# Two x tiles and two slices of w1 as four 128 KB loads, taken up tile by tile at the start of a Mish layer

## The chip, the cores and the metric

The kernel runs on one core of a Trainium2 chip. The metric is the time of one execution on the device, in microseconds (us). The profile is one further execution, recorded by the hardware profiler; its span runs from the first instruction to the last.

## What is computed

```python
B, S, D, F = 1, 2048, 512, 1792          # all bfloat16
def reference(x, w1, b1, w2):
    h = jnp.einsum("bsd,df->bsf", x, w1) + b1
    sp = jnp.log1p(jnp.exp(-jnp.abs(h))) + jnp.where(h > 0, h, jnp.zeros_like(h))
    act = h * jnp.tanh(sp)               # Mish
    return jnp.einsum("bsf,fd->bsd", act, w2)
```

## The kernel before, in words

The two products work on tiles of 128. D is 4 tiles (index k), F is 14 tiles (f), S is 16 tiles of x (i or j) in four blocks of 512 rows (s). For the first product TensorE holds a 128 x 128 piece of w1 as weights and streams a block of x transposed (xT, D on the partitions) past it; four such products, k 0 to 3, add up in one of the eight PSUM banks. ScalarE then applies Mish with the bias b1 (`mish`, L194) and writes `a_sb`. The second product (`mm2`, L245) holds a piece of `a_sb` as weights and streams w2 past it over all 14 f; VectorE copies the result out (L231), SP's queue stores it (L235). VectorE also works out the last six rows of x's first product as dot products (L208).

Everything is ordered by hand. A `Stream` is an engine with a semaphore: `mark` counts up when an instruction ends, and `wait` puts a wait ahead of the engine's next instruction. Each load has a semaphore of its own (`load`, L91 to L94).

The loads are all issued at the top, from two queues. SP issues, in this order: `x_nat` (x tiles 0 and 1 in one load of 256 KB, L129; each partition takes two neighbouring rows of x, 2 KB together), w1's k 2 and 3 for f 0 to 3, w1's k 0 and 1 and then k 2 and 3 for f 4 to 7, a transposing load of x tiles 2 and 3 (L132), w1 for f 8 to 13 in two loads, and then w2, the six rows for VectorE, a transposed copy of w1 and the rest of x by transposing loads. ScalarE's queue issues w1's k 0 and 1 for f 0 to 3 (256 KB, L134), then b1 (L135), and after these the table load for Mish (L150).

x tiles 0 and 1 are transposed on TensorE. While their load is under way, TensorE runs fillers: products of constants into a bank that is not yet used, five of 512 and five of 128 columns (`WARM`, L7; `dummy`, L156). Then `transpose_x` (L163) runs three times: k 0 into bank 6, k 1 into bank 5, k 2 and 3 into bank 4, each for both tiles (eight transposes, L168). After each, VectorE copies the bank into `xT` (L172: 256, 256 and 512 columns). VectorE then turns b1 into a column per f (L256 to L261).

The first products follow (L262 to L265): for f 0 to 3 and then f 4 to 7, over k 0 to 3, products of 256 columns (x tiles 0 and 1) into banks 0 to 7 (`mm1_step`, L190). L266 to L269 add x tiles 2 and 3 for the same eight f and hand each to Mish. Then come f 8 to 13 of block 0 with 512 columns, the second product of block 0, and the same for the other blocks.

Since a partition of `x_nat` holds two neighbouring rows of x, output tiles 0 and 1 are stored through a view with the same interleaving (`out01`, L128 and L234).

Of the kernel before, what the change touches and what calls it, by code (L numbers as in the profile page):

```python
# [4 lines left out]

P = 128
WARM = (512,) * 5 + (128,) * 5  # L7
GROUPS = ((0, 4), (4, 8), (8, 14))
BLOCKS = (512, 512, 512, 512)
LAST = (0, 256, 416, 512)  # L10
# [25 lines left out]
def bass_standalone__dense_activation_mish__prompt_kernel(  # L36
# [10 lines left out]
    BF, F32 = dt.bfloat16, dt.float32  # L47
# [3 lines left out]
    KT, FT = D // P, F // P  # L51
    assert (S, D, F) == (2048, 512, 1792) and sum(BLOCKS) == S
    x2, out2 = x[0], out[0]
# [5 lines left out]
    with ExitStack() as es:  # L59
        def sb(name, shape, t):  # L60
            return es.enter_context(nc.sbuf_tensor(name, shape, t))

        x_nat = sb("x_nat", [P, 2, D], BF)
        xT = sb("xT", [P, KT, S], BF)
# [9 lines left out]
        o_sb = sb("o_sb", [P, S // P, D], BF)  # L74
# [5 lines left out]
        ps = es.enter_context(nc.psum_tensor("ps", [P, 8, 512], F32))  # L80

        def sem(name):
            return es.enter_context(nc.semaphore(name))

        sp = Stream(nc.sync, None)
        pe = Stream(nc.tensor, sem("c_pe"))
        dve = Stream(nc.vector, sem("c_dve"))
        act = Stream(nc.scalar, sem("c_act"))
        pool = Stream(nc.gpsimd, sem("c_pool"))

        def load(q, dst, src, name, transpose=False):  # L91
            s = sem(name)
            (q.eng.dma_start_transpose if transpose else q.eng.dma_start)(dst, src).then_inc(s, 16)
            return (s, 16)  # L94

        t_w1, t_w2, t_xT, t_w1T, t_xv = {}, {}, {}, {}, {}

        def load_w1(q, ks, a, b):
            t = load(q, w1_sb[:, ks, a * P:b * P], w1v[:, ks, a * P:b * P], "s_w1_%d_%d" % (ks.start, a))
            for f in range(a, b):  # L100
                for k in range(ks.start, ks.stop):
                    t_w1[k, f] = t
# [6 lines left out]
        def load_xT(lo, hi):  # L109
            t = load(sp, xT[:, :, lo:hi], x2[lo:hi, :], "s_xT%d" % lo, True)  # L110
            for j in range(lo // P, hi // P):
                t_xT[j] = t
# [11 lines left out]
        t_bz = dve.mark(nc.vector.memset(b1_pad[:, :], 0.0))  # L124
        act.wait(t_bz)

        x01 = x2[0:2 * P, :].rearrange("(p j) d -> p j d", j=2)
        out01 = out2[0:2 * P, :].rearrange("(p j) d -> p j d", j=2)  # L128
        t_xn = load(sp, x_nat[:, :, :], x01, "s_xn")  # L129
        for a, b in GROUPS:  # L130
            if a == F0:
                load_xT(2 * P, 4 * P)  # L132
            for ks in (slice(0, 2), slice(2, KT)):
                load_w1(act if (a, ks.start) == (0, 0) else sp, ks, a, b)  # L134
        t_b1 = load(act, b1_nat[:, :], b1.rearrange("(j p) -> j p", p=P), "s_b1")  # L135
        load_w2(0, 5)
        load_w2(5, FT)
# [5 lines left out]
        for s in range(2, len(BLOCKS)):  # L143
# [4 lines left out]
        t_id = pool.mark(pool.eng.affine_select(ident[:, :], ones[:, :], pattern=[[1, P]], compare_op=ALU.is_equal,  # L148
                                                fill=0.0, base=0, channel_multiplier=-1))
        act.eng.preload_act_table(ACT.Mish)  # L150

        c_w = nc.const_aps.tensor(1.0, [P, P], BF)
        c_m = nc.const_aps.tensor(1.0, [P, 512], BF)

        def dummy(n):
            nc.tensor.matmul(ps[:, 7, 0:n], c_w, c_m[:, 0:n], start=True, stop=True)  # L156

        free = [[] for _ in range(8)]
        t_cp = {}
        t_mish = {}  # L160


        def transpose_x(bank, ks):  # L163
            pe.wait(t_xn, t_id, *free[bank])
            psb = ps[:, bank, :].bitcast(BF)
            for i, k in enumerate(ks):
                for j in range(2):
                    mm = nc.tensor.transpose(psb[:, (2 * i + j) * P:(2 * i + j + 1) * P],  # L168
                                             x_nat[:, j, k * P:(k + 1) * P], ident[:, :])
            n = len(ks)  # L170
            dve.wait(pe.mark(mm))
            t = dve.mark(nc.vector.tensor_copy(xT[:, ks[0]:ks[0] + n, 0:2 * P],  # L172
                                               psb[:, 0:2 * n * P].rearrange("p (k t) -> p k t", k=n)))
            for k in ks:
                t_cp[k] = t
            free[bank] = [t]

        def width(s):
            return BLOCKS[s] - (NV if s == len(BLOCKS) - 1 else 0)

        def mm1_step(s, f, k, bank, j0=0, j1=None):
            j1 = BLOCKS[s] // P if j1 is None else j1
            lo, hi = j0 * P, min(j1 * P, width(s))
            first = k == 0 and j0 == 0
            if first:
                pe.wait(*free[bank])
            pe.wait(t_w1[k, f])
            for j in range(starts[s] // P + j0, starts[s] // P + j1):
                pe.wait(t_cp[k] if j < 2 else t_xT[j])
            return nc.tensor.matmul(ps[:, bank, lo:hi], w1_sb[:, k, f * P:(f + 1) * P],  # L190
                                    xT[:, k, starts[s] + lo:starts[s] + hi], start=first,
                                    stop=(k == KT - 1 and hi == width(s)))
# [28 lines left out]
        s_out = sem("s_out")  # L221
        n_out = 0

        def put(i, lo, hi, bank, t_mm, q):
            nonlocal n_out
            if q is act:
                act.wait(t_mm)
                t = act.mark(act.eng.activation(o_sb[:, i, lo:hi], ps[:, bank, 0:hi - lo], ACT.Copy))  # L228
            else:
                dve.wait(t_mm)  # L230
                t = dve.mark(nc.vector.tensor_copy(o_sb[:, i, lo:hi], ps[:, bank, 0:hi - lo]))  # L231
            free[bank] = [t]
            q.wait(t)
            dst = out01[:, i, lo:hi] if i < 2 else out2[i * P:(i + 1) * P, lo:hi]  # L234
            q.eng.dma_start(dst, o_sb[:, i, lo:hi]).then_inc(s_out, 16)  # L235
            n_out += 1

        t_v = None
# [1 line left out]
        def mm2(i, lo, hi, bank, q=sp):  # L240
            s = max(b for b in range(len(BLOCKS)) if starts[b] <= i * P)
            pe.wait(*free[bank])
            for f in range(FT):
                pe.wait(t_w2[f], t_mish[s, f], t_v if i == S // P - 1 else None)
                mm = nc.tensor.matmul(ps[:, bank, 0:hi - lo], a_sb[:, f, i * P:(i + 1) * P], w2_sb[:, f, lo:hi],  # L245
                                      start=(f == 0), stop=(f == FT - 1))
            put(i, lo, hi, bank, pe.mark(mm), q)


        for n in WARM:  # L250
            dummy(n)
        transpose_x(6, (0,))
        transpose_x(5, (1,))
        transpose_x(4, (2, 3))
        dve.wait(t_b1, t_bz)
        t_b1p = dve.mark(nc.vector.tensor_copy(b1_pad[0:FT, :], b1_nat[:, :]))  # L256
        dve.wait(t_b1p)
# [2 lines left out]
        dve.wait(t_b1t)  # L260
        t_b1c = dve.mark(nc.vector.tensor_copy(b1_sb[:, :], b1_t[:, 0:FT]))  # L261
        for a, b in GROUPS[:2]:  # L262
            for k in range(KT):
                for f in range(a, b):
                    mm1_step(0, f, k, f, 0, 2)  # L265
        for f in range(F0):  # L266
            for k in range(KT):
                mm = mm1_step(0, f, k, f, 2, 4)
            mish(0, f, f, pe.mark(mm))  # L269

        for s in range(len(BLOCKS)):
            for f in range(F0 if s == 0 else 0, FT):
                bank = f % 8 if s == 0 else 4 + f % 4
                for k in range(KT):
                    mm = mm1_step(s, f, k, bank)
                mish(s, f, bank, pe.mark(mm))
            for i in range(starts[s] // P, starts[s + 1] // P):
                if i < S // P - 1:
                    mm2(i, 0, D, i % 4)
                    dots(DOTS[i])  # L280
                    if i == S // P - 3:
                        t_v = mish_v()
                else:
                    for n in range(len(LAST) - 1):
                        mm2(i, LAST[n], LAST[n + 1], (i + n) % 4, act if LAST[n + 1] == D else sp)
# [29 lines left out]
```

## Time and profile before

| | |
|---|---|
| time, median of 3 runs | 105.08 us (104.6 to 105.33) |
| time of the profiled execution | 104.52 us |
| its span | 103.2 us |
| TensorE (PE) busy | 100.1 us, 97% |
| VectorE (DVE) busy | 64.8 us, 63% |
| ScalarE (ACT) busy | 39.1 us, 38% |
| moved by DMA | 10.58 MB |

PE is TensorE's products, PEld its weight loads, which run beside them. A timeline row has the start, the length, the engine, the kernel's line, the operation with what it writes and reads, and how many instructions are merged in it; in brackets stands the idle time ahead of it and what ended that. A chain row has the start, the length and what ran. In the list of groups, the number behind x is the count, then come busy time, mean length in ns, and the idle time ahead. A row of the windows gives the stretch, its length, the busy time of each engine with its count of instructions, then the granted clock of TensorE, the busy share of the 16 DMA engines, and GB/s. A product's length includes the time that it takes to run through the array, so products overlap; their pitch, from start to start, is what counts.

### The profile page before, as it was taken

How to read it: one execution, taken by the hardware profiler on the slowest of the kernel's cores; microseconds unless marked ns; L12 is line 12 of the kernel's file. 1: busy time of each engine (PE TensorE's matmuls, PEld its weight loads, DVE VectorE, ACT ScalarE, POOL GpSimd, SP SyncE). 2: the span in 40 equal slices, each digit the busy share in tenths (PEclk: the TensorE clock that was granted, in tenths of full speed). 3: DMA queues.
4: the chain of work that ended last, by engine and by line, in shares of the span. 5: the costliest groups of instructions: out<-in, count | busy, mean ns of one | idle time of the engine just before them, and what ended most of it. 6: DMA issues, size and time to landing. Idle time of an engine off the chain costs nothing.

```text
span 103.2 us, 1369 instructions
## 1 busy us (share of the span) xinstructions
PE 100.1 (97%) x518; PEld 50.5 (49%) x526; DVE 64.8 (63%) x196; ACT 39.1 (38%) x59; POOL 0.7 (1%) x6
## 2 busy tenths in 40 slices
PE   6999999999999999999999999999999999999992
PEld 2788644444444444444444444444444444444492
DVE  0340000288989999298889999658889999220241
ACT  1306996000037777100007777400005888700100
POOL 2000000000000000000000000000000000000000
DMA  2999999999999100011011000001111000001112
GB/s 32 373 306 348 359 382 197 249 191 224 237 214 297 55 0 6 0 51 48 3 51 51 0 0 0 10 0 51 51 51 51 3 0 0 0 6 51 51 51 51
DMA packets 20931, 10.58 MB, mean 103 GB/s; under 512 B 15292, under 2 KB 20668, under 8 KB 20924
## 3 DMA queue, kind: packets, MB, share of 16 engines
q1 hardware_dynamic: 20480, 10.20, 37.8%
q10 hardware_dynamic: 444, 0.29, 0.9%
q8 instruction: 4, 0.07, 0.3%
q14 instruction: 3, 0.02, 0.1%
HBM read 4.72 MB, written 2.10 MB: 66 GB/s over the span
## 4 chain that ended last, share of the span: by engine, by line
PE 94%; ACT 3%; issue 0%; ACTq 0%
PE ps L245 47%; PE ps L190 44%; ACT a_sb L196 3%; PE ps L156 3%; PE ps L168 1%; ACT o_sb L228 0%; ACTq L28 0%
## 5 line engine op out<-in xcount | busy, mean ns | idle before, releaser
L196 ACT ACTIVATE a_sb<-ps,b_sb 128x512 bf16<-128x512 f32 (+1 forms) x56 | 37.3, 692 | 49.2 <-PE ps L190 49.2
L208 DVE SCALAR_TENSOR_TENSOR prod<-w1T,xv 128x512 f32<-128x512 bf16 x84 | 52.3, 686 | 0.0
L190 PE MATMUL ps<-xT,w_sb 128*128 128x512 bf16 (+2 forms) x253 | 48.8, 352 | 0.2
L245 PE MATMUL ps<-w_sb,a_sb 128*128 128x512 bf16 (+3 forms) x247 | 48.6, 355 | 0.3
L190 PEld LDWEIGHTS ps<-xT,w_sb 128*128 128x128 bf16 x256 | 25.0, 98 | 23.1
L245 PEld LDWEIGHTS ps<-w_sb,a_sb 128*128 128x128 bf16 x252 | 23.6, 98 | 25.2
L231 DVE CAST o_sb<-ps 128x512 bf16<-128x512 f32 (+2 forms) x17 | 11.1, 654 | 31.8 <-PE ps L245 31.8
L208 DVE DVE_READ_ACCUMULATOR prod<-w1T,xv 128x1 f32 x84 | 6.9, 82 | 0.0
L156 PE MATMUL ps<-const-bfloat16-1.0 128*128 128x512 bf16 (+1 forms) x10 | 2.8, 469 | 0.8 <-PEq L300 0.8
L172 DVE COPY xT<-ps 128x256 bf16<-128x256 bf16 (+1 forms) x3 | 0.9, 337 | 3.1 <-PE ps L168 3.1
L219 ACT ACTIVATE a_sb<-hb 128x84 bf16<-128x84 f32 x1 | 0.3, 272 | 6.2 <-DVE hb L216 6.2
L156 PEld LDWEIGHTS ps<-const-bfloat16-1.0 128*128 128x128 bf16 x10 | 1.2, 142 | 2.2 <-issue 2.2
L228 ACT ACTIVATE o_sb<-ps 128x96 bf16<-128x96 f32 x1 | 0.2, 250 | 5.0 <-PE ps L245 5.0
L150 ACT ACT_TABLE_LOAD x1 | 1.3, 1283 | 2.2 <-issue 2.2
L168 PE MATMUL ps<-ident,x_nat 128*128 128x128 bf16 x8 | 0.9, 284 | 0.0
L259 DVE STREAM_TRANSPOSE b_t<-b_pad 32x32 bf16<-32x32 bf16 x4 | 0.8, 202 | 0.1
L168 PEld LDWEIGHTS ps<-ident,x_nat 128*128 128x128 bf16 x8 | 0.7, 136 | 0.3 <-DMA x_nat<-in_x_dram 0.3
L124 DVE MEMSET b_pad<- 32x64 uint32 x1 | 0.1, 112 | 0.9 <-PEq L300 0.9
L256 DVE COPY b_pad<-b_nat 14x128 bf16<-14x128 bf16 x1 | 0.2, 182 | 0.4 <-DMA b_nat<-in_b_dram 0.4
L148 POOL TENSOR_SCALAR_AFFINE_SELECT ident<-ones 128x128 bf16<-128x128 bf16 x1 | 0.3, 292 | 0.1
L216 DVE TENSOR_TENSOR hb<-hv,b_sb 128x84 f32<-128x84 f32 x1 | 0.2, 233 | 0.0
L146 POOL MEMSET ones<- 128x128 bf16 x1 | 0.2, 204 | 0.3 <-POOLq L300 0.3
(5 smaller groups left out, 0.6 us busy)
## 6 DMA issues: line engine op xcount, KB each, us to landing
out_dram<-o_sb SPq DMA_DIRECT2D x15, 128.0 KB, 1.7
w_sb<-in_w_dram SPq DMA_DIRECT2D x1, 1152.0 KB, 10.0
w_sb<-in_w_dram SPq DMA_DIRECT2D x3, 256.0 KB, 4.2
w_sb<-in_w_dram SPq DMA_DIRECT2D x2, 384.0 KB, 5.6
xv<-in_x_dram SPq DMA_DIRECT2D x1, 768.0 KB, 11.6
w_sb<-in_w_dram SPq DMA_DIRECT2D x1, 640.0 KB, 7.2
x_nat<-in_x_dram SPq DMA_DIRECT2D x1, 256.0 KB, 2.8
w_sb<-in_w_dram ACTq DMA_DIRECT2D x1, 256.0 KB, 3.4
```

Of the source, the lines that this page charges most:

```text
L148: t_id = pool.mark(pool.eng.affine_select(ident[:, :], ones[:, :], pattern=[[1, P]], compare_op=ALU.is_equal, fill=0.0, base=0, channel_mu ...
L150: act.eng.preload_act_table(ACT.Mish)
L156: nc.tensor.matmul(ps[:, 7, 0:n], c_w, c_m[:, 0:n], start=True, stop=True)
L168: mm = nc.tensor.transpose(psb[:, (2 * i + j) * P:(2 * i + j + 1) * P], x_nat[:, j, k * P:(k + 1) * P], ident[:, :])
L172: t = dve.mark(nc.vector.tensor_copy(xT[:, ks[0]:ks[0] + n, 0:2 * P], psb[:, 0:2 * n * P].rearrange("p (k t) -> p k t", k=n)))
L190: return nc.tensor.matmul(ps[:, bank, lo:hi], w1_sb[:, k, f * P:(f + 1) * P], xT[:, k, starts[s] + lo:starts[s] + hi], start=first, stop=( ...
L196: t = act.mark(act.eng.activation(a_sb[:, f, starts[s]:starts[s] + width(s)], ps[:, bank, 0:width(s)], ACT.Mish, bias=b1_sb[:, f:f + 1]))
L208: t_dot[b] = dve.mark(nc.vector.scalar_tensor_tensor(prod[:, b, :], w1T[:, f, :], 1.0, xv[:, v, :], ALU.mult, ALU.mult, accum_out=hv[:, f, ...
L219: return act.mark(act.eng.activation(a_sb[:, :, S - NV:S], hb[:, :, :], ACT.Mish))
L231: t = dve.mark(nc.vector.tensor_copy(o_sb[:, i, lo:hi], ps[:, bank, 0:hi - lo]))
L245: mm = nc.tensor.matmul(ps[:, bank, 0:hi - lo], a_sb[:, f, i * P:(i + 1) * P], w2_sb[:, f, lo:hi], start=(f == 0), stop=(f == FT - 1))
L259: t_b1t = dve.mark(nc.vector.transpose(b1_t[c * 32:(c + 1) * 32, :], b1_pad[:, c * 32:(c + 1) * 32]))
```

## The change

The load of x tiles 0 and 1 becomes two loads of 128 KB, one per tile, both on SP; w1's k 0 and 1 for f 0 to 3 become two loads of 128 KB, both on ScalarE's queue. The remaining loads keep their order. A partition of `x_nat` now holds row p of tile j, so `out01` goes.

`transpose_x` works on one tile: it waits for that tile's load, then transposes k 0, k 1, and k 2 and 3 into three banks, and VectorE copies each (128, 128 and 256 columns). Tile 0's goes first, then two fillers of 128 and 64 columns, then the products of f 0 to 3 with k 0 for tile 0 alone (128 columns), then tile 1's transposes, then f 0 to 3 with k 1 for tile 0, k 0 for tile 1 and k 1 for tile 1. From k 2 on, the products have 256 columns as before. Ahead of the first transposes there are two fillers of 128 columns in place of five; the fillers write bank 3 in place of 7.

```diff
-WARM = (512,) * 5 + (128,) * 5
+WARM = (512,) * 5 + (128,) * 2
...
-        x01 = x2[0:2 * P, :].rearrange("(p j) d -> p j d", j=2)
-        out01 = out2[0:2 * P, :].rearrange("(p j) d -> p j d", j=2)
-        t_xn = load(sp, x_nat[:, :, :], x01, "s_xn")
+        t_xn = [load(sp, x_nat[:, j, :], x2[j * P:(j + 1) * P, :], "s_xn%d" % j) for j in range(2)]
...
-            for ks in (slice(0, 2), slice(2, KT)):
-                load_w1(act if (a, ks.start) == (0, 0) else sp, ks, a, b)
+            for ks in (slice(0, 1), slice(1, 2), slice(2, KT)) if a == 0 else (slice(0, 2), slice(2, KT)):
+                load_w1(act if a == 0 and ks.stop <= 2 else sp, ks, a, b)
...
-            nc.tensor.matmul(ps[:, 7, 0:n], c_w, c_m[:, 0:n], start=True, stop=True)
+            nc.tensor.matmul(ps[:, 3, 0:n], c_w, c_m[:, 0:n], start=True, stop=True)
...
-        def transpose_x(bank, ks):
-            pe.wait(t_xn, t_id, *free[bank])
-            psb = ps[:, bank, :].bitcast(BF)
-            for i, k in enumerate(ks):
-                for j in range(2):
-                    mm = nc.tensor.transpose(psb[:, (2 * i + j) * P:(2 * i + j + 1) * P],
+        def transpose_x(j, groups):
+            pe.wait(t_xn[j], t_id)
+            for bank, ks in groups:
+                pe.wait(*free[bank])
+                psb = ps[:, bank, :].bitcast(BF)
+                n = len(ks)
+                for i, k in enumerate(ks):
+                    mm = nc.tensor.transpose(psb[:, i * P:(i + 1) * P],
                                              x_nat[:, j, k * P:(k + 1) * P], ident[:, :])
...
+                dve.wait(pe.mark(mm))
+                t = dve.mark(nc.vector.tensor_copy(
+                    xT[:, ks[0]:ks[0] + n, j * P:(j + 1) * P],
+                    psb[:, 0:n * P].rearrange("p (k t) -> p k t", k=n)))
+                for k in ks:
+                    t_cp[j, k] = t
+                free[bank] = [t]
...
-                pe.wait(t_cp[k] if j < 2 else t_xT[j])
+                pe.wait(t_cp[j, k] if j < 2 else t_xT[j])
...
-            dst = out01[:, i, lo:hi] if i < 2 else out2[i * P:(i + 1) * P, lo:hi]
-            q.eng.dma_start(dst, o_sb[:, i, lo:hi]).then_inc(s_out, 16)
+            q.eng.dma_start(out2[i * P:(i + 1) * P, lo:hi], o_sb[:, i, lo:hi]).then_inc(s_out, 16)
...
-        transpose_x(6, (0,))
-        transpose_x(5, (1,))
-        transpose_x(4, (2, 3))
+        transpose_x(0, ((6, (0,)), (5, (1,)), (4, (2, 3))))
+        dummy(128)
+        dummy(64)
+
+        def first(j, k):
+            for f in range(*GROUPS[0]):
+                mm1_step(0, f, k, f, j, j + 1)
+
+        first(0, 0)
+        transpose_x(1, ((7, (0,)), (6, (1,)), (5, (2, 3))))
+        first(0, 1)
+        first(1, 0)
+        first(1, 1)
...
-            for k in range(KT):
+            for k in range(2 if a == 0 else 0, KT):
```

More of the change, by code (lines that the diff above doesn't have):

```diff
@@ L160, in bass_standalone__dense_activation_mish__prompt_kernel @@
         t_mish = {}
-        def transpose_x(bank, ks):
-            pe.wait(t_xn, t_id, *free[bank])
-            psb = ps[:, bank, :].bitcast(BF)
-            for i, k in enumerate(ks):
-                for j in range(2):
-                    mm = nc.tensor.transpose(psb[:, (2 * i + j) * P:(2 * i + j + 1) * P],
-                                             x_nat[:, j, k * P:(k + 1) * P], ident[:, :])
[L170 to L176, printed above, removed]
+        def transpose_x(j, groups):
[6 more added lines that the diff above has]
+                    mm = nc.tensor.transpose(psb[:, i * P:(i + 1) * P],
+                                             x_nat[:, j, k * P:(k + 1) * P], ident[:, :])
+                dve.wait(pe.mark(mm))
[5 more added lines that the diff above has]
+                free[bank] = [t]
         def width(s):
```

## The prediction

> **What bounds the kernel now.** I read the page first, then the chain of work that ended last over the first 10 us, then the timeline of the start, because the edit touches nothing after about 5.5 us.
>
> ```profile
> span 103.2 us, 1369 instructions
> PE 94%; ACT 3%; issue 0%; ACTq 0%
> ```
>
> ```profile
> 0.84 2.83 PE ps L156 x10
> 3.67 0.01 issue
> 3.67 0.90 PE ps L168 x8
> 4.57 4.08 PE ps L190 x36
> ```
>
> TensorE carries the chain: fillers (L156) to 3.67, the transposes of x tiles 0 and 1 (L168) to about 4.5, and from there matmuls with no gap that matters to the end. So this edit is worth exactly the shift of one moment: when the k 2 products of the first group begin. What follows is the same 256- and 512-column stream in both kernels.
>
> ```profile
> 0.81 0.39 SPq L93 DMA_DIRECT2D x_nat<-in_x_dram  x1
> 1.02 0.43 ACTq L93 DMA_DIRECT2D w_sb<-in_w_dram  x1
> 1.26 1.44 SPq L93 DMA_DIRECT2D w_sb<-in_w_dram  x3
> 1.47 0.71 ACTq L93 DMA_DIRECT2D b_nat<-in_b_dram  x1
> 2.74 1.30 SPq L93 DMA_TRANSPOSE xT<-in_x_dram  x1
> 3.67 0.73 PEld L168 LDWEIGHTS ps<-ident,x_nat 128*128 128x128 bf16 x8 [0.27 <-DMA x_nat<-in_x_dram]
> 4.11 0.93 DVE L172 COPY xT<-ps 128x256 bf16<-128x256 bf16 x3 [3.12 <-PE ps L168]
> 4.54 11.68 PE L190 MATMUL ps<-xT,w_sb 128*128 128x256 bf16 x84
> 5.40 0.18 DVE L256 COPY b_pad<-b_nat 14x128 bf16<-14x128 bf16 x1 [0.36 <-DMA b_nat<-in_b_dram]
> 8.74 7.13 ACT L196 ACTIVATE a_sb<-ps,b_sb 128x512 bf16<-128x512 f32 x12 [5.24 <-PE ps L190]
> ```
>
> The weight loader sits idle 0.27 us for x_nat, up to 3.67. That is the first wait of the chain. The first product starts at 4.54. Times to landing stand in the list of DMA issues, and for three loads that share a line in that list cut to a narrow window:
>
> ```profile
> x_nat<-in_x_dram SPq DMA_DIRECT2D x1, 256.0 KB, 2.8
> w_sb<-in_w_dram ACTq DMA_DIRECT2D x1, 256.0 KB, 3.4
> w_sb<-in_w_dram SPq DMA_DIRECT2D x1, 256.0 KB, 3.9
> w_sb<-in_w_dram SPq DMA_DIRECT2D x1, 256.0 KB, 4.4
> xT<-in_x_dram SPq DMA_TRANSPOSE x1, 4.8
> ```
>
> x_nat lands at 0.81 + 2.8 = 3.61, w1's k 0 and 1 at 1.02 + 3.4 = 4.42, w1's k 2 and 3 at 1.26 + 3.9 = 5.16. The wait for x_nat is followed closely by the next two: w1 at 4.42 is ready only 0.12 before the first product.
>
> Pitches I need, from rows of merged weight loads (one load per product, so the row's length less one load's own time, divided by the steps, is the pitch):
>
> ```profile
> 3.75 0.58 PEld L168 LDWEIGHTS ps<-ident,x_nat 128*128 128x128 bf16 x5
> 4.98 2.06 PEld L190 LDWEIGHTS ps<-xT,w_sb 128*128 128x128 bf16 x19
> 99.68 0.93 PEld L245 LDWEIGHTS ps<-w_sb,a_sb 128*128 128x128 bf16 x13
> 100.58 0.68 PEld L245 LDWEIGHTS ps<-w_sb,a_sb 128*128 128x128 bf16 x14
> L168 PEld LDWEIGHTS ps<-ident,x_nat x8: 105/151/151, 3.7 to 4.3; 128*128 128x128 bf16 x8
> ```
>
> Transposes of 128 columns: (0.58 − 0.15) / 4 = 0.107 us. Later products of 256 columns: (2.06 − 0.10) / 18 = 0.109, of 160: (0.93 − 0.10) / 12 = 0.069, of 96: (0.68 − 0.10 − 0.07) / 12 = 0.043 (its first step is a 160). So 128 columns cost about 0.056 then, half of the transposes' 0.107: TensorE changes from a slow to a fast pace among the last transposes, at about 4.25 (their weight loads go from 151 to 105 ns), though the granted clock reads 1.00 throughout.
>
> **The change part by part.**
>
> *Smaller first load.* Tile 0 of x is 128 KB, half as much. What is half the load worth?
>
> ```profile
> 2.20:2.40 0.20, 0.20 (x2) 0.03 (x1) 0.00 (x0) 0.19 (x1) 0.00 (x0) 1.00 0.08 31
> 2.80:3.00 0.20, 0.20 (x2) 0.07 (x1) 0.00 (x0) 0.20 (x1) 0.00 (x0) 1.00 1.03 399
> 4.80:5.00 0.20, 0.20 (x5) 0.18 (x3) 0.20 (x1) 0.00 (x0) 0.00 (x0) 1.00 1.11 394
> ```
>
> Until 2.40 hardly anything moves (31 GB/s in the slice before), then the engines run at 399 GB/s on x's 2 KB rows and at 394 on w1's 1 KB rows. Bounds: 131 KB at 331 to 399 GB/s is at most about 0.39 us (331 being the window 2.40 to 3.00, below); at least 0, if the slow start were all. On each of 16 engines a tile is 8 rows; the first is the slow start, seven remain, and 2 KB against 1 KB is 0.082 against 0.042 us at these rates: 7 × 0.04 = 0.28. I take 0.27. Tile 0 lands at 3.34, transposes start at 3.40 instead of 3.67.
>
> ```profile
> 2.40:3.00 0.60, 0.60 (x3) 0.22 (x2) 0.00 (x0) 0.60 (x1) 0.00 (x0) 1.00 0.90 331
> ```
>
> *Three fewer fillers ahead.* The last filler before, from the timeline cut to 3.6 to 4.2:
>
> ```profile
> 3.35 0.31 PE L156 MATMUL ps<-const-bfloat16-1.0 128*128 128x128 bf16 x1
> ```
>
> Three fillers of 128 columns at 0.107 are 0.32, so the last one now ends at 3.35 instead of 3.67 and doesn't hold the transposes. Two new ones (128 and 64) behind tile 0's transposes cost 0.16, from 3.81 to 3.97, and lie inside the wait for VectorE's copy. They cost nothing while that wait lasts to 4.09; without it, up to 0.16.
>
> *From tile 0 to the first product.* Copies:
>
> ```profile
> L172 DVE COPY xT<-ps 128x256 bf16<-128x256 bf16 x2 | 0.5, 292 | 3.1 <-PE ps L168 3.1
> L172 DVE COPY xT<-ps 128x512 bf16<-128x512 bf16 x1 | 0.4, 425 | 0.0
> L168 PE MATMUL ps<-ident,x_nat 128*128 128x128 bf16 x8 | 0.9, 284 | 0.0
> ```
>
> From 256 to 512 columns adds 133 ns, so 128 columns cost about 292 − 67 = 225 (bounds 159, the fixed part, and 292). Before, the copy began at 4.11, took 0.29, and the product began 0.14 after it. Now: one transpose, 3.40 + 0.29 + 0.04 = 3.73, copy to 3.95, first product at 4.09. That is 0.45 earlier than 4.54. w1's k 0 must be there by then: it is second in the order of issue, and with tile 0 that makes as many bytes as x_nat had, so it lands near 3.6, at the latest about 3.9: in time.
>
> *Order of the loads.* All SP issues after the first move back by one issue, 0.45 (0.81 to 1.26), and the b1 load on ScalarE's queue by the same. The engines are full from 2.40 on (399, 394 GB/s), so bytes, not issue times, set the landings, and the bytes ahead of each later load are the same. The table load and b1 have cover: b1's chain on VectorE begins at 5.40 and the first Mish is at 8.74. The transposing load of x tiles 2 and 3 lands at 2.74 + 4.8 = 7.54 and is wanted at 4.54 + 32 × 0.109 = 8.03, so even the whole 0.45 would fit. w1's second group (the 4.4 row is its second half, the last of the three issues of the row at 1.26, begun at about 2.23) lands at 2.23 + 4.4 = 6.63 and is wanted at 4.54 + 24 × 0.109 = 7.16.
>
> *The stores of tiles 0 and 1* write the same rows of 1 KB, only to other addresses, and lie behind TensorE's chain, 1.7 us each: nothing.
>
> ```profile
> out_dram<-o_sb SPq DMA_DIRECT2D x15, 128.0 KB, 1.7
> ```
>
> *Sixteen products of 128 columns for eight of 256, tile 1's transposes between them.* The first four start at 4.09, two of them at the slow pace: to 4.42. Then tile 1's four transposes at 0.056: to 4.64. Tile 1 is third in the queue, 131 KB at 394 GB/s (0.33) behind w1's k 0, so it lands at 3.95 to 4.2; TensorE waits for it in front of all that follows, so each 0.1 after 4.42 would cost 0.1. w1's k 1 is fourth and lands where the whole load did, at 4.42, and is wanted at 4.64. VectorE's three copies start at 4.42 + 0.22 + 0.04 = 4.68 and take 0.225 + 0.225 + 0.29 (k 2 and 3, 256 columns) = 0.74, to 5.42. TensorE's own work, twelve products at 0.056, would be through at 4.64 + 0.67 = 5.31, but k 2 needs the third copy and the 0.14 behind it: **5.56**. Before, k 2 began at 4.54 + 8 × 0.109 = **5.41**. The loss is 0.15.
>
> So the sum: 0.27 from the load and 0.18 from the shorter first transposing and copying (together 0.45); less 0.33 for four products ahead of tile 1 (two of them slow), less 0.22 for tile 1's transposes, which now stand between, less 0.92 from there to k 2 (0.04 + 0.74 + 0.14), against 0.87 before for eight products: 0.45 − 0.33 − 0.22 − 0.92 + 0.87 = **−0.15**, a loss. The wait that goes (x_nat's second half) comes back as six copies in a row on VectorE.
>
> The profiled execution took 104.52 around its span of 103.2; with the loss 104.67. It is 0.56 under the median of the three runs, 105.08, so the forecast is 105.08 + 0.15, or **105.2**.
>
> **The rivals.**
>
> *The copies don't hold, the load pays in full (gain).* If tile 0 lands 0.39 earlier and the copies cost their lower bound of 0.16 for 128 columns, TensorE alone sets the end: first product at 3.28 + 0.29 + 0.04 + 0.16 + 0.14 = 3.91, its four at the slow pace to 4.33 (tile 1 is in by then), k 2 at 4.33 + 0.22 + 0.67 = 5.22. It can't be much earlier: w1's k 2 and 3 land at 5.16. Gain 0.2: 104.9. For it speaks that tile 0 is a short load; against it the 292 ns row of the copy.
>
> *The order of landing (loss).* If tile 1 goes ahead of w1's k 0, or the 0.45 later issue on SP tells, w1's k 0 lands as late as the whole load did, 4.42, and the first product is back at 4.54. Then tile 1's transposes, copies and all follow 0.45 later: 105.08 + 0.15 + 0.45 = 105.7. The transfers by queue speak against it:
>
> ```profile
> q10 hardware_dynamic: 110, 0.11, 105.4%
> q1 hardware_dynamic: 4, 0.00, 0.8%
> ```
>
> From 3.2 to 3.5 ScalarE's queue (q10) had the engines to itself, although SP's next load had been issued at 1.26: the loads were taken whole, in order of issue. [...]
>
> *The pace of TensorE comes later (slower than before).* In the trace the slow pace ends about 3.4 us after the first filler, which ran almost without pause. Before, the filler begun at 3.35 could have had a successor at 3.46, and TensorE took in nothing until 3.67; another 0.12 went ahead of 4.54. The change leaves it without work from 3.46 − 0.32 = 3.14 to 3.40, and again from 3.97 to 4.09: 0.38 in place of 0.33. If idle time in this stretch postpones the fast pace by D, each us costs half a us of work: D = 3.4 again costs 1.7, and the run takes 106.9. Against it: 0.05 more idle is little beside 3.4. [...]
>
> **How the numbers follow.** The likeliest, 0.55: 105.2. The gain, 0.20: 104.9. The order of landing, 0.15: 105.7. The late pace, 0.10: up to 106.9, half of it under 106.1. The three runs spread 0.73 (104.6 to 105.33), so half of that goes around the outer cases: 104.9 − 0.37 gives about 104.4 and 105.7 + 0.37 about 106.1. A measurement of this kernel can tell about 1%, here 1.05 us, from no change. A gain of that size is shut out by w1's k 2 and 3 at 5.16: faster 0.03, for noise. Slower by over 1% needs D over 1.8: 0.08. Within 1%: 0.89.
>
> **What would show it.** Right: transposes begin near 3.4, the first 128-column product near 4.1, tile 1's transposes near 4.4, the first k 2 product near 5.55 behind a wait of L190 for VectorE's copy; from there every later group about 0.15 later than before. Wrong: a first product at 4.4 or later with a wait for w_sb (order of landing); k 2 at or before 5.3 (the gain); products after 4.5 still at 0.107 for 128 columns (pace); or a new wait after 6 us, which would mean that the later issues on SP do tell.

## The result, and the profile after

| | before | changed |
|---|---|---|
| time, median of 22 runs each | 104.72 us (104.37 to 105.52) | 105.63 us (105.14 to 107.86) |
| profiled execution / span | 104.52 / 103.2 us | 105.63 / 104.4 us |
| ratio | | **1.0067**, 95% interval 1.0044 to 1.0091 |

The change makes the kernel slower by 0.7 us (0.0067 × 104.72; 0.46 to 0.95 by the interval). The ratio is lower than that of the medians, in part because it leaves out five executions of the changed kernel that took about 107 us or more, none of them profiled.

The page of the changed kernel, its first line and the chain's shares by engine:

```profile
span 104.4 us, 1388 instructions
PE 90%; DMA 4%; ACT 3%; issue 1%; ACTq 0%; DVE 0%
```

A transfer has entered the chain. In order of time (start, length, what ran):

```profile
1.02 0.38 ACTq L93
1.39 0.03 issue
1.42 3.92 DMA w_sb<-in_w_dram
5.35 0.05 issue
5.39 4.41 PE ps L190 x40
```

Until 5.39 the end of the kernel hangs on a single load, the one issued on ScalarE's queue at 1.42: w1's k 1. Fillers and transposes, which led the chain before, are gone from it. The list of waits has what was not there before:

```profile
PEld ps L190 <- DMA w_sb<-in_w_dram: 0.8, 1, 0.8
PE ps L190 <- DMA w_sb<-in_w_dram: 0.5, 1, 0.5
```

And the timeline of the start, to be read against the one in the prediction:

```profile
0.81 0.87 SPq L93 DMA_DIRECT2D x_nat<-in_x_dram  x2
1.02 0.86 ACTq L93 DMA_DIRECT2D w_sb<-in_w_dram  x2
1.72 1.45 SPq L93 DMA_DIRECT2D w_sb<-in_w_dram  x3
3.04 0.46 PEld L168 LDWEIGHTS ps<-ident,x_nat 128*128 128x128 bf16 x4
3.49 0.61 DVE L171 COPY xT<-ps 128x128 bf16<-128x128 bf16 x3 [2.51 <-PE ps L168]
3.86 0.59 PE L190 MATMUL ps<-xT,w_sb 128*128 128x128 bf16 x4
4.14 0.47 PEld L168 LDWEIGHTS ps<-ident,x_nat 128*128 128x128 bf16 x4
4.59 0.61 DVE L171 COPY xT<-ps 128x128 bf16<-128x128 bf16 x3 [0.49 <-PE ps L168]
5.39 1.16 PEld L190 LDWEIGHTS ps<-xT,w_sb 128*128 128x128 bf16 x12 [0.78 <-DMA w_sb<-in_w_dram]
```

The front of it works better than forecast: the first product starts at 3.86, 0.68 ahead of before. Then everything that was won stands still in front of w1's k 1. VectorE's copies are through at 5.20, ahead of it. The time to landing of each of the first five loads, from the list of issues cut to narrow windows, in order of issue (0.81, 1.02, 1.26, 1.42, 1.72):

```profile
x_nat<-in_x_dram SPq DMA_DIRECT2D x1, 128.0 KB, 2.2
w_sb<-in_w_dram ACTq DMA_DIRECT2D x1, 128.0 KB, 2.3
x_nat<-in_x_dram SPq DMA_DIRECT2D x1, 128.0 KB, 2.4
w_sb<-in_w_dram ACTq DMA_DIRECT2D x1, 128.0 KB, 3.9
w_sb<-in_w_dram SPq DMA_DIRECT2D x1, 256.0 KB, 4.1
```

Landings: 3.0, 3.3, 3.7, 5.3, 5.8. The first three come early, the fourth is 0.9 behind the 4.42 at which the undivided load landed before, and the fifth 0.6 behind 5.16. The rate of the engines over the time between (last column GB/s, ahead of it the busy share of the engines), first the changed kernel, then before:

```profile
2.40:3.00 0.60, 0.60 (x3) 0.22 (x2) 0.00 (x0) 0.39 (x1) 0.00 (x0) 1.00 1.08 369
3.00:3.60 0.60, 0.60 (x8) 0.60 (x7) 0.11 (x1) 0.60 (x1) 0.00 (x0) 1.00 1.04 200
3.60:4.20 0.60, 0.60 (x8) 0.49 (x7) 0.50 (x3) 0.29 (x1) 0.00 (x0) 1.00 0.87 216
```

```profile
3.00:3.60 0.60, 0.60 (x6) 0.40 (x4) 0.00 (x0) 0.49 (x1) 0.00 (x0) 1.00 1.04 357
3.60:4.20 0.60, 0.59 (x7) 0.53 (x7) 0.10 (x1) 0.00 (x0) 0.00 (x0) 1.00 1.09 379
```

The engines are nearly as busy as before and move little more than half as much. Single packets show how. Of the 243 packets of 1 KB, a row each, that began from 3.0 to 4.2, most took 46 ns, as before, but 25 took over 100 ns, up to 1.07 us, and these 25 hold 7.8 of the 18.1 us that all of them took together. Before, 3 of 405 took over 100 ns, at most 0.25 us. So a few packets stall, and the others go at their old pace. That stretch, 1.2 us at 200 to 216 GB/s, is where w1 falls behind.

A second loss lies behind the wait. The twelve weight loads from 5.39 span 1.16, a pitch of about 0.1, the slow pace; the k 2 products follow only then. The row that ends with the first k 2 weight load, in the changed kernel and then before:

```profile
6.43 0.17 PEld L190 LDWEIGHTS ps<-xT,w_sb 128*128 128x128 bf16 x2
```

```profile
5.31 0.10 PEld L190 LDWEIGHTS ps<-xT,w_sb 128*128 128x128 bf16 x1
```

6.43 + 0.17 − 0.10 = 6.50 against 5.31, 1.19 later, and the spans differ by 1.2: all that follows is shifted and nothing else. That is the difference between two executions; over all runs it is 0.7.

### The profile page after: what moved, and what is told of

It reads as the page before. It is cut to its first block, busy times and chain, and to the rows that moved or that the text cites. A ratio compares the mean times of both kernels' runs of the same rounds, so it can differ in the third digit from the quotient of the medians.

```text
span 104.4 us, 1388 instructions
## 1 busy us (share of the span) xinstructions
PE 100.8 (97%) x525; PEld 51.2 (49%) x533; DVE 65.2 (62%) x199; ACT 39.1 (37%) x59; POOL 0.7 (1%) x6
## 4 chain that ended last, share of the span: by engine, by line
PE 90%; DMA 4%; ACT 3%; issue 1%; ACTq 0%; DVE 0%
PE ps L244 46%; PE ps L190 44%; DMA w_sb<-in_w_dram 4%; ACT a_sb L196 3%; ACTq L93 0%; ACT o_sb L228 0%; DVE b_pad L124 0%; ACTq L28 0%
## 5 line engine op out<-in xcount | busy, mean ns | idle before, releaser
L190 PE MATMUL ps<-xT,w_sb 128*128 128x512 bf16 (+3 forms) x261 | 49.7, 351 | 0.7 <-DMA w_sb<-in_w_dram 0.5
L190 PEld LDWEIGHTS ps<-xT,w_sb 128*128 128x128 bf16 x264 | 25.7, 100 | 23.8 <-DMA w_sb<-in_w_dram 0.8
L154 PE MATMUL ps<-const-bfloat16-1.0 128*128 128x512 bf16 (+2 forms) x9 | 2.9, 481 | 0.8 <-PEq L309 0.8
L171 DVE COPY xT<-ps 128x128 bf16<-128x128 bf16 (+1 forms) x6 | 1.2, 244 | 3.0 <-PE ps L168 3.0
```

The source lines that it names most:

```text
L154: nc.tensor.matmul(ps[:, 3, 0:n], c_w, c_m[:, 0:n], start=True, stop=True)
L171: t = dve.mark(nc.vector.tensor_copy(xT[:, ks[0]:ks[0] + n, j * P:(j + 1) * P], psb[:, 0:n * P].rearrange("p (k t) -> p k t", k=n)))
```

## The experiments

The theory after the result: w1's k 1, and k 2 and 3 behind it, land late because of how the loads are cut and issued, and TensorE waits for them (**landing**). The rivals: TensorE's slow pace, lasting longer because of the idle time (**pace**); the new order of the work itself, as forecast (**order**); and **chance**, one stall in one execution.

**The changed kernel, profiled again** (no edit).

> The changed kernel, profiled once more. Theory (landing): w1's k 1, the second load on ScalarE's queue, lands late every time, at 5.0 us or later, and the first k 1 product starts 0.05 behind it; the wait for w_sb is 0.3 to 0.8 us again. Rival (chance): the late landing was one stall in one execution; here k 1 lands at 4.0 to 4.5 and no wait for w_sb is over 0.1. Rival (pace): the slow pace ends at another moment than 6.3 us, and the time moves with it by half the difference.

```profile
span 104.1 us, 1388 instructions
```

```profile
5.13 0.73 PEld L190 LDWEIGHTS ps<-xT,w_sb 128*128 128x128 bf16 x12 [0.53 <-DMA w_sb<-in_w_dram]
6.25 0.11 PEld L190 LDWEIGHTS ps<-xT,w_sb 128*128 128x128 bf16 x2 [0.39 <-DMA w_sb<-in_w_dram]
```

```profile
3.00:4.80 1.80, 1.80 (x17) 1.49 (x15) 0.82 (x5) 0.89 (x1) 0.00 (x0) 1.00 0.84 243
```

Chance falls: k 1 is late again (1.42 + 3.7 = 5.1), and k 2 and 3 too (1.72 + 4.5 = 6.2). This time the pace was fast from about 5.3 on (twelve loads in 0.73, a pitch of 0.057), the products were done by about 5.85, and TensorE waited a second time, for k 2 and 3. One execution pays with a wait and slow products behind it, the other with two waits: k 2's first weight load is at 6.50 in the one and 6.25 in the other.

**w1's k 0 and 1 in one load again**, x in two:

```diff
-            for ks in (slice(0, 1), slice(1, 2), slice(2, KT)) if a == 0 else (slice(0, 2), slice(2, KT)):
-                load_w1(act if a == 0 and ks.stop <= 2 else sp, ks, a, b)
+            for ks in (slice(0, 2), slice(2, KT)):
+                load_w1(act if (a, ks.start) == (0, 0) else sp, ks, a, b)
```

> The change with w1's k 0 and k 1 left in one load of 256 KB on ScalarE's queue; x stays in two loads. Landing theory: the whole load lands at 3.7 to 4.2, the first product starts at 3.9 to 4.3 and nothing waits behind it, so the time is 0.5 to 0.8 under the change, within 0.2 of before (ratio 0.998 to 1.002). Pace rival: the loss came from the pace and the idle time, which one landing doesn't cure: ratio 1.004 or more.

1.0033 (1.0001 to 1.0064): about half of the loss goes, less than expected, and the interval overlaps the change's. The whole load lands at 1.02 + 3.2 = 4.2, so the first product waits for it, and x tile 1 comes only at 1.26 + 3.3 = 4.6, behind it in the order of issue. A slow stretch is there as well, earlier and shorter:

```profile
2.40:3.00 0.60, 0.60 (x3) 0.22 (x2) 0.00 (x0) 0.60 (x1) 0.00 (x0) 1.00 0.71 145
```

But it costs w1 little: from 1.80 to 4.80 the engines moved 284 GB/s here, 301 and 290 in the two profiles of the kernel before, and 256 in the changed kernel's first. What is left of the loss is not this stretch: the first product waits for the whole load, tile 1 comes behind it, and the pace was slow to about 5.6 (an estimate: the 41 weight loads from 4.96 on span 4.12, where 12 steps of 0.057, 28 of 0.109 and a load of 0.10 make 3.84; the 0.28 over it is five or six products at 0.107 in place of 0.057).

**More fillers in the wait for k 1**:

```diff
-        def dummy(n):
-            nc.tensor.matmul(ps[:, 3, 0:n], c_w, c_m[:, 0:n], start=True, stop=True)
+        def dummy(n, bank=3):
+            nc.tensor.matmul(ps[:, bank, 0:n], c_w, c_m[:, 0:n], start=True, stop=True)
...
+        pe.wait(*free[4])
+        for _ in range(7):
+            dummy(128, 4)
         first(0, 1)
```

> The change with seven more fillers of 128 columns (0.75 us at the slow pace) between tile 1's transposes and the first k 1 product, so that TensorE isn't idle while it waits for w1's k 1. Landing theory: k 1 still lands when it does, the first k 1 product starts at the same moment, and the ratio stays at 1.005 to 1.008. Pace rival: without the idle stretch the fast pace comes by 4.5 to 5, the twelve products cost 0.67 in place of 1.2, and the time falls by 0.5 (ratio 1.001 to 1.003), and single runs over 106.5 vanish.

1.0058 (1.0031 to 1.0085), as landing had it. TensorE loads weights until 5.4 and still finds k 1 missing, which landed at 1.42 + 4.2 = 5.6:

```profile
5.66 3.34 PEld L190 LDWEIGHTS ps<-xT,w_sb 128*128 128x128 bf16 x35 [0.30 <-DMA w_sb<-in_w_dram]
```

The pace was slow all the same: the weight loads of the seven fillers, from 4.56, span 0.79, a pitch of 0.107 up to 5.35. So idle time ahead of k 1 is not the cause of the loss, and keeping TensorE at work did not bring the fast pace sooner here than the 5.3 of the second profile without it. Of the twelve executions none took over 105.9; twelve are too few to say that the fillers did that.

**k 1 on SP**, behind x tile 1:

```diff
-                load_w1(act if a == 0 and ks.stop <= 2 else sp, ks, a, b)
+                load_w1(act if a == 0 and ks.stop <= 1 else sp, ks, a, b)
```

> The change with w1's k 1 load issued on SP, behind x tile 1 and ahead of w1's k 2 and 3; ScalarE's queue keeps k 0 and b1. Landing theory: one queue serves its loads in order, so k 1 lands at 4.0 to 4.4 and k 2 and 3 at 4.8 to 5.2; the wait for w_sb goes and the ratio to before is 0.998 to 1.002. Rival (VectorE's six copies in a row bound it, as predicted): k 2 begins about 5.55 and the ratio is 1.001 to 1.003. Rival (the engines are simply slow there): k 1 lands at 5 or later here too.

1.0021 (0.9995 to 1.0046), just above the theory's numbers and among those of VectorE's copies, but the way of neither: the copies end at 5.19 and hold nothing up, k 1 lands at 1.71 + 3.1 = 4.8 and k 2 and 3 at 2.18 + 3.5 = 5.7, and k 2's first weight load follows after 5.72. From 3.0 to 4.8 the engines moved only

```profile
3.00:4.80 1.80, 1.80 (x17) 1.48 (x15) 0.83 (x5) 0.41 (x1) 0.00 (x0) 1.00 0.83 225
```

The slow stretch is there, 130 GB/s from 3.6 to 4.2, though ScalarE's queue has only k 0, in at 1.02 + 2.2 = 3.2, and the 3.5 KB of b1. So it isn't two queues moving w1 at the same time.

**The split of w1 alone** (the loop of the change's diff, in the kernel before):

> The kernel before with only w1's k 0 and k 1 as two loads of 128 KB on ScalarE's queue; x in one load, TensorE's order as before. Theory (the split of w1 slows w1): k 1 lands at 4.8 to 5.4 in place of 4.41, k 2 and 3 at 5.5 to 6.2 in place of 5.13, and the ratio is 1.003 to 1.007. Rival (the split of x does it): k 1 lands at 4.4 to 4.5, k 2 and 3 at 5.1 to 5.2, ratio 0.999 to 1.001.

1.0028 (0.9996 to 1.006), inconclusive as a time. The landings tell more: k 2 and 3, issued at 1.26, came at 4.7, ahead of k 1, issued at 1.42, at 5.0: in order of issue. The rate from 3.0 to 4.8 was 320 GB/s; the deep stretch is missing, though from 4.2 to 4.8 the rate fell to 258.

```profile
3.00:4.80 1.80, 1.80 (x16) 1.44 (x15) 0.61 (x3) 0.89 (x1) 0.00 (x0) 1.00 1.01 320
```

**The split of x alone** (the `t_xn` line of the change; TensorE in the order of before, waiting for both tiles):

> The kernel before with only x tiles 0 and 1 as two loads of 128 KB on SP (1 KB rows); w1 in one load, TensorE's order as before and waiting for both tiles. Theory (the split of w1): x tile 1 lands at 3.6 to 3.7, w1 at 4.4 to 4.5, k 2 and 3 at 5.1 to 5.2, ratio 0.999 to 1.002. Rival (the split of x): w1's load has slow packets from 2.3 to 4.4, lands at 4.5 to 5, k 2 and 3 at 5.3 to 6, ratio 1.002 to 1.006.

1.0126 (1.006 to 1.0193), far outside both. Neither had reckoned with the order of issue: tile 1 (issued at 1.26) lands behind the 256 KB of w1 (issued at 1.02), at 1.26 + 3.2 = 4.5, and the transposes of both tiles wait for it.

```profile
4.52 0.78 PEld L166 LDWEIGHTS ps<-ident,x_nat 128*128 128x128 bf16 x8 [1.12 <-issue]
L188 PEld LDWEIGHTS ps<-xT,w_sb 128*128 128x128 bf16 x16 | 2.3, 146 | 0.9
```

The second row, the weight loads from 5.4 to 8.5, averages 146 ns: slow until 8.5. The profiled execution took 106.97 and the six from 105.32 to 107.34, so the pace need not be as late in each. In the change, the split of w1 is what brings tile 1 in at 3.7: the two splits need each other. In every run here these first loads were issued from the two queues in turn, so the order of landing is shown for that pattern of issue alone.

**x in one load, but 1 KB rows**:

```diff
-        x01 = x2[0:2 * P, :].rearrange("(p j) d -> p j d", j=2)
-        out01 = out2[0:2 * P, :].rearrange("(p j) d -> p j d", j=2)
+        x01 = x2[0:2 * P, :].rearrange("(j p) d -> p j d", j=2)
...
```

> The kernel before with x tiles 0 and 1 in one load of 256 KB as before, but tile by tile in each partition, so that it moves 1 KB rows in place of 2 KB. Theory (the split of w1): x lands at 3.6 to 3.7 and all else as before, ratio 0.999 to 1.001. Rival (the rows of x, not the number of loads): x's first packets take about 0.2 in place of 0.4 to 0.57 us, and w1's packets are slow right behind them; w1 lands at 4.5 or later, ratio 1.002 to 1.006.

1.0014 (0.9986 to 1.0042); x lands at 0.80 + 2.7 = 3.5, w1 at 1.01 + 3.3 = 4.3, k 2 and 3 at 1.30 + 4.0 = 5.3, with 339 GB/s from 3.0 to 4.8. The row length alone isn't it.

**No fillers** in the kernel before (`WARM = ()`):

> The kernel before without any filler: TensorE is idle until x_nat has landed, 3.67. It measures what a later fast pace costs. [...] Rival (the pace doesn't depend on the fillers): it changes at 4.3 as before and the ratio is 0.998 to 1.001.

1.0132 (1.0078 to 1.0186). The first product starts where it did, but weight loads average 143 ns from 4.45 to 6.35 and 98 from 6.6:

```profile
L190 PEld LDWEIGHTS ps<-xT,w_sb 128*128 128x128 bf16 x10 | 1.4, 143 | 0.6
```

```profile
L190 PEld LDWEIGHTS ps<-xT,w_sb 128*128 128x128 bf16 x14 | 1.4, 98 | 0.2
```

The fast pace comes about 2.1 later than at 4.25, and the span grows from 103.2 to 104.1: 0.9, near the half that the prediction put on each us. The profiled execution, 105.39, is among the fastest of six; the slowest took 106.74.

**The order alone** (the change's TensorE and VectorE order; x in one load, w1 in one load, five fillers ahead):

> TensorE's and VectorE's order of the change (tile by tile, six copies, sixteen products of 128 columns) with the loads of before: x in one load (1 KB rows), w1's k 0 and 1 in one load, five fillers of 128 columns ahead. It measures the step that the prediction gave 0.15 us. Theory (landing): the order alone costs 0.1 to 0.3 us, ratio 1.001 to 1.003, and nothing waits for w_sb over 0.1. Rival (the order is the loss): ratio 1.005 or more.

1.0017 (0.9991 to 1.0044), that is 0.18 us: the theory's number, and the prediction's 0.15, though the interval also holds no change at all. w1 landed at 4.4 and was waited for:

```profile
3.58 0.23 PEld L168 LDWEIGHTS ps<-ident,x_nat 128*128 128x128 bf16 x4 [0.19 <-DMA x_nat<-in_x_dram]
4.47 0.23 PEld L190 LDWEIGHTS ps<-xT,w_sb 128*128 128x128 bf16 x4 [0.56 <-DMA w_sb<-in_w_dram]
```

The second wait is longer than the 0.1 of the theory, because two tiles that arrive together leave nothing to do ahead of w1. So the run tests the new order, but with a wait for w1 ahead of the copies that the forecast had as the bound.

**The bytes in the order of before, x still in two loads** (tile 0 on SP, tile 1 on ScalarE's queue, w1 whole on SP behind; products of 256 columns):

```diff
-        t_xn = [load(sp, x_nat[:, j, :], x2[j * P:(j + 1) * P, :], "s_xn%d" % j) for j in range(2)]
+        t_xn = [load((sp, act)[j], x_nat[:, j, :], x2[j * P:(j + 1) * P, :], "s_xn%d" % j) for j in range(2)]
...
+            for ks in (slice(0, 2), slice(2, KT)):
+                load_w1(sp, ks, a, b)
...
```

> x in two loads as in the change, but issued side by side (tile 0 on SP, tile 1 on ScalarE's queue), w1's k 0 and 1 in one load on SP behind them, the products of 256 columns as before. So the order of the bytes is that of before. Theory (loads land in order of issue): tile 1 lands at 3.3 to 3.7, w1 at 4.2 to 4.5, the first product starts at 4.3 to 4.6, ratio 0.998 to 1.001. Rival (a first load of 128 KB brings slow packets to w1 whatever the order): a stretch under 250 GB/s between 2.4 and 4.2, w1 at 4.6 or later, ratio 1.002 to 1.006.

1.0042 (1.0012 to 1.0072), the rival's number, but neither's way there: no 0.6 us from 2.4 to 4.2 is under 250 GB/s, and w1's k 0 and 1 land at 1.26 + 2.9 = 4.2, as the theory had it. It is k 2 and 3, third on SP, that come late, at 1.72 + 4.6 = 6.3:

```profile
3.60:4.20 0.60, 0.59 (x8) 0.38 (x6) 0.60 (x5) 0.00 (x0) 0.00 (x0) 1.00 0.95 259
4.20:4.80 0.60, 0.42 (x4) 0.41 (x5) 0.56 (x5) 0.00 (x0) 0.00 (x0) 1.00 0.87 265
4.80:5.40 0.60, 0.60 (x6) 0.29 (x4) 0.51 (x4) 0.00 (x0) 0.00 (x0) 1.00 0.94 266
```

```profile
6.36 0.77 PEld L190 LDWEIGHTS ps<-xT,w_sb 128*128 128x128 bf16 x8 [1.23 <-DMA w_sb<-in_w_dram]
```

**The kernel before, profiled again** (no edit).

> The kernel before, profiled once more. Theory (the change makes w1 late): w1's k 2 and 3 land at 5.1 to 5.3 again and 200 GB/s or less isn't seen between 2.4 and 4.8. Rival (the first profile of before was a lucky one): a stretch under 250 GB/s before 4.8 and k 2 and 3 at 5.5 or later. The fast pace comes at another moment than 4.25, and the time differs by half of that.

```profile
3.00:4.80 1.80, 1.80 (x17) 1.52 (x16) 0.70 (x3) 0.49 (x1) 0.00 (x0) 1.00 1.05 335
```

k 2 and 3 at 1.26 + 3.8 = 5.1 again, 335 GB/s, nothing waits for w_sb. The first profile wasn't a lucky one. The fast pace came about 0.3 later than in the first, near 4.6, with the same program: the 38 weight loads up to 8.5 span 4.17 in place of 4.06, and 0.11 is what one product of 256 columns at twice 0.107 adds to its 0.109.

**One more load on SP, x in one load**: 8 KB that nobody reads, issued behind x_nat in the kernel before, so that k 2 and 3 are issued at 1.72.

```diff
+        scratch = sb("scratch", [P, 32], BF)
...
         t_xn = load(sp, x_nat[:, :, :], x01, "s_xn")
+        load(sp, scratch[:, :], x2[0:P, 0:32], "s_scratch")
```

> The kernel before with one more load on SP behind x_nat, 8 KB that nobody reads (128 rows of 64 B), so that w1's k 2 and 3 and all that follows on SP is issued 0.45 us later, as in the change, with x still in one load. Theory (two loads of x make w1's packets slow): k 2 and 3 land at 5.1 to 5.3, no stretch under 250 GB/s before 4.8, ratio 0.999 to 1.001. Rival (the later issue on SP, or one more load in the queue, does it): k 2 and 3 land at 5.5 or later, a stretch under 250 GB/s between 3.0 and 4.8, ratio 1.003 or more.

```profile
3.60:4.20 0.60, 0.60 (x7) 0.56 (x7) 0.13 (x1) 0.00 (x0) 0.00 (x0) 1.00 1.08 226
4.20:4.80 0.60, 0.60 (x8) 0.47 (x6) 0.59 (x3) 0.00 (x0) 0.00 (x0) 1.00 0.94 241
```

```profile
6.09 0.77 PEld L192 LDWEIGHTS ps<-xT,w_sb 128*128 128x128 bf16 x8 [0.83 <-DMA w_sb<-in_w_dram]
```

The profile is the rival's: x undivided, and yet the slow stretch, k 2 and 3 at 1.72 + 4.3 = 6.0, and TensorE waiting. The time is the theory's: 0.9996 (0.9969 to 1.0023). The profiled execution, 105.24, is the slowest of twelve from 104.52 on, so the stretch may not come in each of them. What it rules out is that x in two loads is necessary for a slow stretch: this execution had one without them. That the small load brought it is not shown by one profile.

## Why the prediction was right in its direction and wrong in its size

The forecast was a small loss, 0.15 us; the loss is 0.70. That it is a loss was forecast for a reason, VectorE's copies, that did not hold anything up, so the direction came out right by luck. The time, 105.63 against 105.2, is also nearer than the working deserves: the forecast started from a median of three runs, 105.08, which stands 0.36 above the 104.72 of all 22.

*One moment sets the end*: right. In the first profile k 2's first weight load moved by 1.19 and the span by 1.2, and in the second profile by 0.94 (6.25 − 5.31) and 0.9.

*Smaller first load, 0.27*: mis-sized. Tile 0 landed at 3.0 in place of 3.61, 0.6 earlier, more than the upper bound of 0.39. That bound took the slow start as given; the engines moved 212 GB/s from 1.80 to 2.40 in the changed kernel:

```profile
1.80:2.40 0.60, 0.60 (x3) 0.15 (x1) 0.00 (x0) 0.00 (x0) 0.00 (x0) 1.00 0.70 212
```

Before they had moved 65 in that stretch. In six profiles with x in two loads it is 174 to 230, in five with x in one load 65 to 157. The transposes then waited for the last filler's slot more than for the load: in the second profile tile 0 landed 0.1 earlier, at 0.81 + 2.1 = 2.9, and their weight loads began at 3.03 against 3.04. The first product came at 3.86, not 4.09.

*The order of the work, a loss*: the number fits, the reason is not borne out. Done alone it cost 0.18 us, forecast 0.15, in an interval that holds no change too, and there the first product waited 0.56 for w1. In the changed kernel VectorE's six copies, the reason given, hold nothing up: they end at 5.20, before k 1's products begin.

*Order of the loads*: **this step failed**. "Bytes, not issue times, set the landings, and the bytes ahead of each later load are the same" put w1's k 1 at 4.42 and k 2 and 3 at 5.16. They landed at 5.3 and 5.8, and at 5.1 and 6.2. The bytes are the same, but the engines do not hold their 394 GB/s. The six profiles in which w1's k 2 and 3 are the second load on SP moved 320 to 370 GB/s from 3.0 to 4.8 and have that load in by 5.3. Of the eight in which another load is ahead of it on SP, six moved 215 to 290 there and have it in at 5.7 to 6.3. The division is not as clean as that sounds: the other two of the eight (w1 in one load on ScalarE's queue, x in two) had a stretch of 145 and 162 from 2.4 to 3.0, but moved 357 and 358 from 3.0 to 4.8 and have the load in at 5.3; only the six fell behind. The forecast's rival of the order of landing had "the 0.45 later issue on SP tells" in it, with a chance of 0.15, but looked for the lateness in k 0, which came early.

*From there to the sum*, in the first profile. Tile 1's transposes ended where they were forecast: their weight loads were through at 4.61, forecast 4.64. The copies, which hold nothing up, give back 5.56 − 5.31 = 0.25. The wait for k 1, from the forecast 4.64 to 5.39, adds 0.75. The slow pace adds 0.45 (twelve products from 5.39 to 6.51 in place of 0.67). So 5.56 − 0.25 + 0.75 + 0.45 = 6.51, as the trace has it.

*The late pace*, a rival: the pace came at about 6.4 in the first profile and at about 5.3 in the second, with the same program, and at 4.25 and near 4.6 in the two of the kernel before. So the program alone does not set it; whether the change makes it later on the average is not shown. The transposes of the order-alone kernel ran fast at 3.58, only 2.7 us after the first filler, so "3.4 us after the first filler" is a reading of one trace and no rule. The 106.9 was worked out from a delay of 3.4, which no run shows as such: where the pace came later than 4.25, it was by 0.3 to 4.2, and 2.1 later cost 0.9 in the kernel without fillers.

**What stays open** is why single packets stall. Three things are not needed for a slow stretch or do not bring it. One came with x undivided (226 GB/s from 3.6 to 4.2), so two loads of x are not needed. One came with k 1 on SP, when ScalarE's queue had nothing of w1 left to move (k 0 in at 3.2, 130 GB/s from 3.6 to 4.2), so two queues moving w1 at the same time are not needed. And 1 KB rows of x in one load did not bring it (339 GB/s from 3.0 to 4.8). The kernels that fell behind share a further load on SP ahead of w1's k 2 and 3, but not every kernel with such a load fell behind, and the run that added just that had the stretch in its profile and no loss over its executions. So it is not settled.

No kernel here beats the one before.

## What to carry to other kernels

A transfer that is cut in two to get its first half earlier also puts another load into the queue. Here the loads of x and w1 landed in order of issue, over both queues, so the second half stands behind whatever the other queue issued in between (x tile 1, issued at 1.26, landed at 3.7 behind 128 KB of w1 and at 4.5 behind 256 KB). When the loads run one behind the other at full rate (357 to 381 GB/s from 3.0 to 5.4 in the kernel before), list what each later load is wanted for and how much slack it has (at most 0.25 us for w1's k 2 and 3 here) before the first one is made faster. And where TensorE starts at a slow pace that ends at another moment from one execution to the next (about 6.4 and 5.3 in two profiles of the changed kernel), one profile is not enough to read a difference of half a us.

## What the runs showed of the hardware that was not expected

- The first load of a kernel landed 2.1 to 2.2 us after its issue with 128 KB and 2.7 to 2.8 with 256 KB: 0.6 apart, though 128 KB at the 331 to 399 GB/s measured behind it take 0.3 to 0.4.
- The moment at which TensorE's pace doubles lay anywhere from before 3.58 to 8.5 us in these profiles, with the granted clock at 1.00 over each run. Coming 2.1 us later cost 0.9 us.
- Products of 128 columns, each with its own weight load, follow at 0.057 us in the fast pace, so cutting 256 columns (0.109) in two costs next to nothing then.
- The DMA engines can be busy at a share of 0.87 to 1.04 and move 200 to 216 GB/s (the changed kernel, 3.0 to 4.2), with 1 KB rows that at other moments go at 394: most packets still take 46 ns, but one in ten takes over 100 ns, up to 1.07 us.
